# Attention scores on quarters of the PE array, queries and keys loaded as token x both heads, value copies on GpSimd

## The chip, the cores and the metric

One core of a Trainium2 chip runs the whole program in one launch. The metric is the device time of that launch in microseconds (us), the median of several runs. Five engines work from queues of their own, in order: TensorE (matmuls and transposes, into PSUM), VectorE and ScalarE (which empty PSUM and do the elementwise work), GpSimd (elementwise work in SBUF) and SyncE (SP), which here issues nearly all DMA transfers. PSUM has eight banks of 2 KB per partition. Semaphores tie the queues together; a buffer that is used again is such a tie too.

## The reference

Three parts follow one another; the change is in the first.

```python
def _attn_ref(q, k, v):                    # (4, 8, 576, 64) each, fp32
    scores = (1.0 / np.sqrt(D)) * np.matmul(q, k.transpose(0, 1, 3, 2))
    rel = pos[:, None] - pos[None, :]
    scores = np.where((rel >= 0) & (rel < 64), scores, -1e9)
    scores = scores - np.max(scores, axis=-1, keepdims=True)
    attn = np.exp(scores)
    attn = attn / (np.sum(attn, axis=-1, keepdims=True) + 1e-09)
    return np.matmul(attn, v)
```

Then 2304 tokens of 512 values are routed to 8 experts with 288 places each (two products with a ReLU between), and the result goes through a gated product with 1536 inner columns.

## The kernel before, in words

**Units and groups.** The window of 64 means that a block of 64 queries needs two blocks of 64 keys. A unit (b, c, hp) is one block c of 64 queries (nine in a sequence) of two heads, hp and hp + 4, in batch b. There are 144 units in the order batch, head pair, block, and four make a group g (36 groups). One turn i of the main loop (from line 346 on) does one step for each of several groups: scores(i), maxima(i), exponents(i-1), transposed(i-3), values(i-5), out_x(i-6), the preparations that a plan gives to this turn (take(i)), norms(i-1). Inside norms(i-1) stands negated(i), the negated maxima which the next exponentials need as a bias. The order of the lines is the order of each engine's queue.

**Loads and preparation.** load_rows brings 576 rows of queries or keys of both heads as 72 partitions with two tokens side by side. prep turns one head's rows with four transposes into a tile ps_t and copies it out with two copies of 64 partitions (even and odd tokens): keys on ScalarE into kt (L196), queries on VectorE (L198) into qbd, in which the two heads of a unit stand on the diagonal, with zeros beside them. load_v brings values to partitions 64 to 127 of vw, and copy_v moves them by DMA to partitions 0 to 63, one block later (L177), so that one matmul meets the previous and the present block of keys.

**Scores to outputs.** scores writes the mask (a matmul of 512 columns with the identity, L206) and adds four products of 128x128x128 (L210; in fp32 one product is two instructions). maxima is a reduction on VectorE (L216), exponents are four exponentials on ScalarE with sums (L226), norms are small operations on VectorE (L231, L219, L234) and a product on GpSimd (L238), transposed are four transposes into a ps_t tile (L243) and a copy on ScalarE (L251). values are eight products into two halves of the output's partitions (L259), out_x copies the outputs to xT on VectorE (L273). When 512 tokens of all heads are there, logits (L283, four column strips of the array) and logits2 (L295) make the routing's inputs.

**PSUM.** ps_s has two banks (scores), ps_t three (transposed probabilities and preparations, by turns), ps_o two (outputs), ps_l one (logits).

**The plan.** todo gives each half of a preparation its turn, at most two in a turn; loads gives each head pair's load its turn, by when buffers come free (three for raw queries and keys, six for vw). At the end of turn 27 (`if i == 3 * NC`) convert_move and st.load(4) issue seven loads of weights of 512 KB, on the same SP queue.

Of the kernel before, what the change touches and what calls it, by code (L numbers as in the profile page):

```python
# [7 lines left out]
F32 = mybir.dt.float32  # L8
# [60 lines left out]
class Kernel:  # L69
# [30 lines left out]
    def attention(self, ctx):  # L100
# [45 lines left out]
        def qbd(b, hp):  # L146
            return qbds[(b * HP + hp) % NQ]


        vws = [one.tile([128, NC, 2, D], F32, name=f"vw{i}") for i in range(NV)]  # L150
# [5 lines left out]


        units = [(b, c, hp) for b in range(B) for hp in range(HP) for c in range(NC)]
        groups = [units[4 * g:4 * g + 4] for g in range(len(units) // 4)]
        NG = len(groups)  # L160

        raw, kt = {}, {}
# [16 lines left out]
        def prep(name, b, hp, s):  # L179


            ps = ps_t.tile([128, 4, 72], F32, name="ps_t")
            for t in range(4):
                nc.tensor.transpose(ps[:, t, :], raw[name, b, hp][:, s, t], self.ident[0:72, 0:72])
            sl = slice(64 * s, 64 * s + 64)
            if name == "k":
                if not s:
                    kt[b, hp] = kt_p.tile([128, NC, 64], F32, name="kt")
                dst = kt[b, hp][sl]
            else:  # L190
                dst = qbd(b, hp)[sl, :, s, :]
            dst = dst.rearrange("r c (m e) -> r e c m", e=2)
            for e in range(2):
                x = ps[64 * e:64 * e + 64].rearrange("r t p -> r (t p)").rearrange("r (c m) -> r c m", c=NC)
                if name == "k":
                    nc.scalar.activation(dst[:, e], x, AF.Copy)  # L196
                else:
                    nc.vector.tensor_copy(dst[:, e], x)  # L198

        SS, PP, PN, PT, OO, SM = {}, {}, {}, {}, {}, {}  # L200

        def scores(g):
            ps = ps_s.tile([128, 4, 128], F32, name="ps_s")
            SS[g] = ps
            first = [4 - u for u, (b, c, hp) in enumerate(groups[g]) if c == 0] or [0]
            mm(ps, identb, mask[:, first[0]:first[0] + 4], start=True, stop=False)  # L206
            for u, (b, c, hp) in enumerate(groups[g]):
                k = kt[b, hp].rearrange("p c i -> p (c i)")
                kk = k[:, 64 * c - 64:64 * c + 64] if c else k[:, None, 0:64].to_broadcast([128, 2, 64])
                mm(ps[:, u, :], qbd(b, hp)[:, c].rearrange("p s i -> p (s i)"), kk, start=False, stop=u == 3)  # L210

# [40 lines left out]

        def values(g, late=False):
            ps = ps_s.tile([128, 4, 64], F32, name="ps_s") if late else ps_o.tile([128, 4, 64], F32, name="ps_o")
            OO[g] = ps
            for u, (b, c, hp) in enumerate(groups[g]):
                for s in range(2):
                    sl = slice(64 * s, 64 * s + 64)
                    mm(ps[sl, u, :], vw(b, hp)[:, c, s, :], PT[g][:, u, 64 * s:64 * s + 64],  # L259
                       start=True, stop=True)  # L260

        def out_x(g, late=False):
            ps, us = OO[g], groups[g]
            u = 0
            while u < 4:
                b, c, hp = us[u]
                n = 1
                while u + n < 4 and us[u + n] == (b, c + n, hp):
                    n += 1
                t0 = b * S + 64 * c  # L270
                dst = xT[:, hp, t0:t0 + 64 * n].rearrange("p (n i) -> p n i", n=n)
                if late:
                    nc.vector.tensor_copy(dst, ps[:, u:u + n])  # L273
                else:
                    nc.scalar.activation(dst, ps[:, u:u + n], AF.Copy)
                u += n

        LT = {}

        def logits(t0, n, ps_p=ps_l, name="ps_l", act=False):  # L280
# [9 lines left out]
        def logits2(t0, n, ps_p=ps_l, name="ps_l"):  # L290
            lt = LT[t0]
# [9 lines left out]
        def load(h):  # L301

            if h < NP:
                load_rows("q", h // HP, h % HP)
                load_rows("k", h // HP, h % HP)
            if 0 < h <= NP:
                load_v((h - 1) // HP, (h - 1) % HP)
            if 1 < h:
                copy_v((h - 2) // HP, (h - 2) % HP)

# [12 lines left out]
        for h in reversed(range(NP)):  # L323
            for a in (("k", 1), ("q", 1), ("k", 0), ("q", 0)):
                i = h * NC // 4 - 2 if h else -1
                if h == 1:
                    i = 0 if a[1] else -1
                while i > 0 and len(todo.get(i, ())) >= 2:
                    i -= 1
                todo.setdefault(max(i, -1), []).insert(0, (h, a))  # L330
        todo[-1].sort(key=lambda x: (x[0], x[1][1]))
        ready = {h: max(i for i, t in todo.items() for x in t if x[0] == h) for h in range(NP)}
        loads = {}
        for h in range(NR, NP + 2):

            i = max(ready[h - NR] if h < NP else 0, (h - NV) * NC // 4 + VL + 1 if h > NV else 0)
            loads.setdefault(i + 1, []).append(h)

        def take(i):
            for h, (name, s) in todo.get(i, ()):  # L340
                prep(name, h // HP, h % HP, s)

        warm = ps_l.tile([128, 512], F32, name="ps_l")
        self.warm(warm, 8)
        take(-1)
        done, late, window = 0, None, iter(())
        for i in range(NG - 1):
            for h in loads.get(i, ()):
                load(h)
            scores(i)  # L350
            maxima(i)
# [8 lines left out]
            if i >= VL + 1:  # L360
                if late:
                    logits2(*late)
                    if late[0] + late[1] == 128 * self.n0:
                        window = self.first_window(ps_l.tile([128, 1], F32, name="ps_l"))
                    late = None
                elif done < 1536 and S * ((i - VL - 1) // NC) >= done + 512:
# [13 lines left out]

        n = NG - 1
        list(window)
        scores(n)
        maxima(n)
        exponents(n - 1)
        negated(n)
        out_x(n - 6, True)
        norms(n - 1)
        transposed(n - 3, True)
        values(n - 5)  # L390
        exponents(n)
        out_x(n - 5, True)
        values(n - 4)
        norms(n, True)
        transposed(n - 2)
        values(n - 3, True)
        out_x(n - 4, True)
        transposed(n - 1)
        out_x(n - 3, True)
        transposed(n, 2)  # L400
        values(n - 2, True)
        values(n - 1)
        out_x(n - 2)
        out_x(n - 1, True)
        values(n)
        out_x(n)
# [4 lines left out]
        logits2(2048, 256)  # L411

# [735 lines left out]
```

## Time and profile before

| what | value |
|---|---|
| time, median of 3 runs | 842.52 us (841.31 to 843.17) |
| profiled execution: its own time | 840.74 us |
| its span | 839.0 us |
| granted TensorE clock, mean over the span | 0.981 |
| TensorE busy | 801.5 us (96%) |
| VectorE busy | 516.9 us (62%) |
| ScalarE busy | 396.3 us (47%) |
| GpSimd busy | 94.9 us (11%) |

The attention stage is the first 122 us of the span or so. The shares of the table are means over stages with different limits, so that stage has to be read by itself: first the busy time by stretch, then the engines' instructions in order of time. A row of the timeline has the start, the time until the last of its instructions ended, the engine, the line, the operation, the tile written and read, the shape, the count and, in brackets, idle time before it with what ended it. PE is TensorE, PEld its weight load, ACT ScalarE, DVE VectorE, POOL GpSimd.

### The profile page before, as it was taken

Reading aid. Unit: us, or ns where it says so; the run is one execution under the profiler, and the core shown is the slowest. Engines: PE = TensorE matmul, PEld = TensorE weight load, DVE = VectorE, ACT = ScalarE, POOL = GpSimd, SP = SyncE. Lnnn points to the kernel's source line nnn. Section 1 sums busy time; section 2 is a strip of 40 time slices with the busy share of each in tenths; the row PEclk is TensorE's granted clock in tenths of the full one; section 3 lists DMA queues with packets and bytes.
Section 4 is the critical chain, followed back from the end, with each engine's and each line's share of the span. In section 5 each row is a group of like instructions: output and inputs, shape, how many; then the busy total and the mean of one; then the engine's idle time right before and its main releaser. Section 6 shows DMA issues by size and latency. Waiting matters only on the chain.

```text
span 839.0 us, 14875 instructions
## 1 busy us (share of the span) xinstructions
PE 801.5 (96%) x5635; PEld 750.0 (89%) x5635; DVE 516.9 (62%) x1104; ACT 396.3 (47%) x998; POOL 94.9 (11%) x167
## 2 busy tenths in 40 slices
PE   7999986599999999999999999999999999999997
PEld 6888965499999999999888989999999999999996
DVE  6777868667777777788787844554443464443432
ACT  5989966346665665664343413433232243231311
POOL 6333323300000000000000000110000002000002
PEclk8999997699999999999999999999999999999999
DMA  8999916657877777786655322232112223201001
GB/s 185 194 190 202 261 49 219 195 167 249 258 263 241 251 239 235 242 240 200 221 159 172 100 103 75 101 126 77 36 41 76 75 87 140 71 15 67 1 1 75
DMA packets 92333, 123.72 MB, mean 147 GB/s; under 512 B 24417, under 2 KB 59233, under 8 KB 92257
## 3 DMA queue, kind: packets, MB, share of 16 engines
q1 hardware_dynamic: 89376, 113.28, 45.5%
q0 software_dynamic: 2880, 9.44, 3.2%
q8 instruction: 46, 0.75, 0.4%
q14 instruction: 31, 0.25, 0.1%
HBM read 99.63 MB, written 18.87 MB: 141 GB/s over the span
## 4 chain that ended last, share of the span: by engine, by line
PE 38%; issue 33%; DVE 6%; POOL 2%; ACT 1%; DMA 1%; POOLq 0%; DVEq 0%
PE psw L943 12%; PE psa L943 12%; PE psg L943 9%; PE pso L943 4%; DVE wlo L60 2%; POOL out_dram L1079 1%; PE psw L975 1%; DVE t L898 1%; DVE t L896 1%; DVE sg L1059 1%; DVE t L900 1%; ACT p L1061 1%; DVE sg L1056 1%; DVE t L894 0%; DMA wraw<-in_moe_w_dram 0%
## 5 line engine op out<-in xcount | busy, mean ns | idle before, releaser
L943 PE MATMUL psg<-y,whi 128*128 128x384 f32 x1152 | 223.1, 336 | 0.0
L943 PEld LDWEIGHTS psg<-y,whi 128*128 128x128 f32 x1152 | 201.6, 188 | 0.0
L60 DVE TENSOR_TENSOR wlo<-wraw,whi 128x512 fp32r<-128x512 f32 x236 | 149.7, 687 | 8.8 <-DVEq L674 3.8
L943 PE MATMUL pso<-whi,p 128*128 128x512 f32 x432 | 133.3, 390 | 0.0
L59 ACT ACTIVATE whi<-wraw 128x512 fp32r<-128x512 f32 x236 | 129.9, 620 | 2.9 <-ACTq L674 2.9
L943 PE MATMUL psg<-y,wlo 128*128 128x384 f32 x576 | 124.1, 337 | 4.4 <-DVE sg L1056 4.4
L1061 ACT ACTIVATE p<-sg 128x384 fp32r<-128x384 f32 x72 | 37.8, 525 | 161.5 <-DVE sg L1059 161.5
L943 PEld LDWEIGHTS psg<-y,wlo 128*128 128x128 f32 x576 | 102.2, 188 | 9.1 <-DVE sg L1056 6.5
L1056 DVE TENSOR_TENSOR sg<-sg,psg 128x384 f32<-128x384 f32 x72 | 39.8, 553 | 107.9 <-ACT sg L1055 107.8
L1055 ACT ACTIVATE sg<-psg 128x384 f32<-128x384 f32 x72 | 35.3, 490 | 134.2 <-PE psg L943 134.2
L943 PEld LDWEIGHTS pso<-whi,p 128*128 128x128 f32 x432 | 80.6, 188 | 14.5
L943 PE MATMUL pso<-wlo,p 128*128 128x512 f32 x216 | 84.2, 390 | 0.0
L943 PE MATMUL psw<-xt,whi 128*128 128x288 f32 x512 | 78.5, 295 | 0.0
L943 PE MATMUL psa<-hh,whi 128*128 128x288 f32 x256 | 75.5, 295 | 0.0
L943 PE MATMUL psa<-hl,whi 128*128 128x288 f32 x256 | 75.5, 295 | 0.0
L943 PE MATMUL psa<-hh,wlo 128*128 128x288 f32 x256 | 75.3, 294 | 0.0
L1059 DVE TENSOR_TENSOR sg<-sg,psg 128x384 f32<-128x384 f32 x72 | 39.9, 555 | 54.7 <-PE psg L943 53.1
L943 PEld LDWEIGHTS psw<-xt,whi 128*128 128x128 f32 x512 | 71.5, 188 | 0.0
L1079 POOL DMA_INDIRECT out_dram<-orow,idx x18 | 17.5, 972 | 461.0 <-ACT orow L1077 270.9
L1062 DVE TENSOR_TENSOR p<-sg,p 128x384 fp32r<-128x384 f32 x72 | 40.2, 559 | 42.6 <-ACT p L1061 42.6
L932 ACT ACTIVATE hh<-psw 128x288 fp32r<-128x288 f32 x64 | 26.3, 411 | 61.8 <-PE psw L943 60.5
L226 ACT ACTIVATE pp<-ps_s,nm 128x128 f32<-128x128 f32 x144 | 50.9, 365 | 5.0 <-DVE nm L219 4.2
(176 smaller groups left out, 1097.4 us busy)
## 6 DMA issues: line engine op xcount, KB each, us to landing
wraw<-in_moe_w_dram SPq DMA_DIRECT2D x64, 512.0 KB
wraw<-w SPq DMA_DIRECT2D x54, 512.0 KB
w<-t SPq DMA_DIRECT2D x36, 256.0 KB
raw<-in_moe_w_gate_dram SPq DMA_DIRECT2D x12, 512.0 KB
raw<-in_moe_w_val_dram SPq DMA_DIRECT2D x12, 512.0 KB
raw<-in_moe_w_out_dram SPq DMA_DIRECT2D x12, 512.0 KB
rawq<-in_q_dram SPq DMA_DIRECT2D x32, 144.0 KB
rawk<-in_k_dram SPq DMA_DIRECT2D x32, 144.0 KB
```

The costliest lines, as they stand in the source:

```text
L59: self.nc.scalar.activation(h[sl], t[sl], AF.Copy)
L60: self.nc.vector.tensor_tensor(lo[sl], t[sl], h[sl].bitcast(F32), op=OP.subtract)
L226: nc.scalar.activation(PP[g][:, u, :], ps[:, u, :], AF.Exp, bias=nm[:, u:u + 1], scale=scale, accum_out=SM[g][:, u:u + 1])
L896: nc.vector.scalar_tensor_tensor(t, hi, -0x40000000, t, op0=OP.bitwise_and, op1=OP.bitwise_or)
L932: nc.scalar.activation(h, x, AF.Relu)
L943: self.nc.tensor.matmul(acc, x, y, start=start and i == 0, stop=stop and i == len(seq) - 1)
L1055: nc.scalar.activation(sg, pg, AF.Sigmoid)
L1056: nc.vector.tensor_tensor(sg, sg, pg, op=OP.mult)
L1059: nc.vector.tensor_tensor(sg, sg, pv, op=OP.mult)
L1061: nc.scalar.activation(p[0][:, sl], sg, AF.Copy)
L1062: nc.vector.tensor_tensor(p[1][:, sl], sg, p[0][:, sl].bitcast(F32), op=OP.subtract)
L1079: d = nc.gpsimd.indirect_dma_start(out=self.out, out_offset=bass.IndirectOffsetOnAxis(ap=self.idx[:, 6 * g + t:6 * g + t + 1], axis=0), in ...
```

## The change

Scores are made for eight units (two groups) at a time, on a quarter of the array each: one head's 64 rows by one block's 64 queries. The two heads go to two PSUM banks, and a group g now holds one head of eight units, two in its partitions. qbd with its zeros is gone. A raw tile has 96 partitions and per token both heads' 64 values, so that one transpose of 96 tokens gives both heads; a preparation is half a sequence: three transposes and one copy of 128 partitions, on VectorE but for the second half of the keys, on ScalarE. Value copies are three GpSimd products with 1.0 per head pair. values and out_x work on eight units, in odd and even turns. ps_s has four banks, ps_t two, ps_o two with the logits among its tiles; vw has five buffers. The end after the loop is written anew. The core of the diff:

```diff
-        NR, NQ, NV, VL = 3, 4, 6, 5
+        NR, NV = 3, 5
-        ps_s, ps_t, ps_o, ps_l = pool("ps_s", 2, PS), pool("ps_t", 3, PS), pool("ps_o", 2, PS), pool("ps_l", 1, PS)
+        ps_s, ps_t, ps_o = pool("ps_s", 4, PS), pool("ps_t", 2, PS), pool("ps_o", 2, PS)
-        qbds = [one.tile([128, NC, 2, 64], F32, name=f"qbd{i}") for i in range(NQ)]
-        for i in range(NQ):
-            for s in range(2):
-                nc.gpsimd.memset(qbds[i][64 * s:64 * s + 64, :, 1 - s], 0.0)
...
-            t = raw[name, b, hp] = raw_p.tile([72, 2, 4, 2 * D], F32, name="raw" + name)
+            t = raw[name, b, hp] = raw_p.tile([96, 6, 2, D], F32, name="raw" + name)
             for s in range(2):
-                nc.sync.dma_start(t[:, s], src[b, HP * s + hp].rearrange("(t p e) d -> p t (e d)", p=72, e=2))
+                nc.sync.dma_start(t[:, :, s, :], src[b, HP * s + hp].rearrange("(t p) d -> p t d", p=96))
...
-        def copy_v(b, hp):
-            nc.sync.dma_start(vw(b, hp)[0:64, 1:NC], vw(b, hp)[64:128, 0:NC - 1])
+        def copy_v(b, hp, i):
+            v, c0, c1 = vw(b, hp), 3 * i + 1, min(3 * i + 4, NC)
+            nc.gpsimd.tensor_tensor(v[0:64, c0:c1], v[64:128, c0 - 1:c1 - 1],
+                                    vone[64:128].to_broadcast([64, c1 - c0, 2, D]), op=OP.mult)
+        def prep(name, b, hp, x):
+            if name == "v":
+                copy_v(b, hp, x)
+                return
+            if not x:
+                tr[name, b, hp] = kt_p.tile([128, S], F32, name=name + "t")
+            ps = ps_t.tile([128, 3, 96], F32, name="ps_t")
+            for t in range(3):
+                nc.tensor.transpose(ps[:, t, :], raw[name, b, hp][:, 3 * x + t].rearrange("p s d -> p (s d)"),
+                                    self.ident[0:96, 0:96])
+            dst = tr[name, b, hp][:, 288 * x:288 * x + 288].rearrange("p (t i) -> p t i", t=3)
+            if name == "k" and x:
+                nc.scalar.activation(dst, ps, AF.Copy)
             else:
+                nc.vector.tensor_copy(dst, ps)
+        def scores(G):
+            us = units[8 * G:8 * G + 8]
+            for h in range(2):
+                SS[2 * G + h] = ps_s.tile([128, 4, 128], F32, name="ps_s")
+            for r in range(2):
+                first = ([4 - m for m in range(4) if us[2 * m + r][1] == 0] or [0])[0]
+                for h, sl in enumerate(sides):
+                    mm(SS[2 * G + h][sides[r]], identb[sl, sl], mask[sl, first:first + 4], start=True, stop=False)
+            for m in range(4):
+                for r in range(2):
+                    b, c, hp = us[2 * m + r]
+                    for h, sl in enumerate(sides):
+                        k = tr["k", b, hp][sl]
+                        kk = k[:, 64 * c - 64:64 * c + 64] if c else k[:, None, 0:64].to_broadcast([64, 2, 64])
+                        mm(SS[2 * G + h][sides[r], m, :], tr["q", b, hp][sl, 64 * c:64 * c + 64], kk,
+                           start=False, stop=m == 3)
+        def values(G, j0=0, n=8, p=ps_o, name="ps_o"):
+            ps = OO[G, j0] = p.tile([128, n, 64], F32, name=name)
+            for j in range(j0, j0 + n):
+                b, c, hp = units[8 * G + j]
+                for h, sl in enumerate(sides):
+                    mm(ps[sl, j - j0, :], vw(b, hp)[:, c, h, :], PT[2 * G + h][:, j // 2, sides[j % 2]],
                        start=True, stop=True)
...
-                i = h * NC // 4 - 2 if h else -1
-                if h == 1:
-                    i = 0 if a[1] else -1
+                i = 2 * ((h * NC + 4 * a[1]) // 8) - (1 if h < 2 else 2)
                 while i > 0 and len(todo.get(i, ())) >= 2:
                     i -= 1
                 todo.setdefault(max(i, -1), []).insert(0, (h, a))
...
+        for h in range(NP):
+            for x in range(3):
+                todo.setdefault(min(2 * ((h * NC + 3 * x) // 8) + 1, NG - 2), []).append((h, ("v", x)))
-        for h in range(NR, NP + 2):
-            i = max(ready[h - NR] if h < NP else 0, (h - NV) * NC // 4 + VL + 1 if h > NV else 0)
+        for h in range(NR, NP + 1):
+            i = max(ready[h - NR] if h < NP else 0, 2 * (((h - NV) * NC - 1) // 8) + 6 if h > NV else 0)
             loads.setdefault(i + 1, []).append(h)
...
-            scores(i)
+            if i % 2 == 0:
+                scores(i // 2)
             maxima(i)
             if i >= 1:
                 exponents(i - 1)
...
             if i >= 3:
                 transposed(i - 3)
-            if i >= VL:
-                values(i - VL)
+            if i % 2 and i >= 5:
+                values((i - 5) // 2)
+            if late:
+                logits2(*late)
...
+            if i % 2 == 0 and i >= 6:
+                if done < 1536 and S * (8 * (i - 6) // 2 // (HP * NC)) >= done + 512:
                     late = (done, 512)
                     logits(*late)
                     done += 512
-                out_x(i - VL - 1, True)
+                out_x((i - 6) // 2)
             take(i)
```

out_x copies on VectorE in both versions of the loop; after the loop the scores of the last group are not made any more, since those of two groups are made in turn 34, and values and out_x of the last 16 units go in halves of four units.

## Rows read from the trace of the kernel before

**Rows 1.** Busy time by stretch: us, PE, PEld, DVE, ACT, POOL, clock, DMA, GB/s.
```profile
84.00:106.30 22.30, 21.70 (x286) 19.53 (x285) 18.52 (x65) 21.43 (x88) 8.32 (x8) 1.00 0.91 252
```
**Rows 2.** Timeline of TensorE, one turn: start, us, engine, line, operation.
```profile
61.99 0.38 PE L206 MATMUL ps_s<-mask,identb 128*128 128x512 bf16 x1 [0.22 <-ACT pp L226]
62.21 1.05 PE L210 MATMUL ps_s<-kt,qbd 128*128 128x128 f32 x8
63.10 0.60 PE L243 MATMUL ps_t<-ident,pn 128*128 128x128 f32 x4
63.63 0.69 PE L259 MATMUL ps_o<-pt,vw 128*64 128x64 f32 x16
64.25 0.47 PE L184 MATMUL ps_t<-ident,rawq 72*128 72x72 f32 x4
...
64.80 0.38 PE L206 MATMUL ps_s<-mask,identb 128*128 128x512 bf16 x1
```
**Rows 3.** Timeline of ScalarE, one turn (exponentials two and three left out).
```profile
60.44 0.37 ACT L226 ACTIVATE pp<-ps_s,nm 128x128 f32<-128x128 f32 x1 [0.33 <-DVE nm L219]
...
61.83 0.60 ACT L251 ACTIVATE pt<-ps_t 128x512 f32<-128x512 f32 x1
62.30 0.87 ACT L196 ACTIVATE kt<-ps_t 64x288 f32<-64x288 f32 x2
63.20 0.37 ACT L226 ACTIVATE pp<-ps_s,nm 128x128 f32<-128x128 f32 x1
```
**Rows 4.** Timeline of VectorE in the same turn.
```profile
61.56 0.92 DVE L198 COPY qbd<-ps_t 64x288 f32<-64x288 f32 x2
62.41 0.15 DVE L231 TENSOR_SCALAR sm<-sm 128x4 f32<-128x4 f32 x1
62.47 0.16 DVE L219 TENSOR_SCALAR nm<-nm 128x4 f32<-128x4 f32 x1
```
**Rows 5.** Timeline of the start: fifth preparation, last one ahead of the loop, first mask.
```profile
7.30 0.33 PEld L184 LDWEIGHTS ps_t<-ident,rawq 72*128 72x128 f32 x4 [0.30 <-ACT kt L196]
...
8.96 0.71 PE L184 MATMUL ps_t<-ident,rawk 72*128 72x72 f32 x4 [1.18 <-DMA rawk<-in_k_dram]
...
9.47 0.63 PE L206 MATMUL ps_s<-mask,identb 128*128 128x512 bf16 x1
```
**Rows 6.** Timeline of ScalarE: first exponential of groups 3, 31, 32 and 34.
```profile
21.82 0.37 ACT L226 ACTIVATE pp<-ps_s,nm 128x128 f32<-128x128 f32 x1
...
104.80 0.37 ACT L226 ACTIVATE pp<-ps_s,nm 128x128 f32<-128x128 f32 x1
...
106.75 0.37 ACT L226 ACTIVATE pp<-ps_s,nm 128x128 f32<-128x128 f32 x1
...
113.42 0.37 ACT L226 ACTIVATE pp<-ps_s,nm 128x128 f32<-128x128 f32 x1 [0.43 <-DVE nm L219]
```
**Rows 7.** Timeline of TensorE: the third logits of the loop.
```profile
108.60 1.07 PE L283 MATMUL ps_l<-big,wgp 128*32 128x512 f32 x8
```
**Rows 8.** Groups by line, 18.2 to 112.5 us: busy us, mean ns, idle before.
```profile
L238 POOL TENSOR_TENSOR pn<-pp,sm 128x512 f32<-128x512 f32 x32 | 33.3, 1039 | 59.4 <-DVE sm L234 30.4 <-PE ps_s L210 14.1 <-PE ps_t L243 4.4
...
L288 DVE COPY lt<-ps_l 128x512 f32<-128x512 f32 x3 | 2.1, 691 | 4.2 <-PE ps_l L283 4.2
```
**Rows 9.** DMA packets and share of 16 engines, 44.2 to 45.2 and 23.1 to 24.1 us.
```profile
DMA packets 310, 0.16 MB, mean 159 GB/s; under 512 B 73, under 2 KB 304, under 8 KB 310
q1 hardware_dynamic: 310, 0.16, 82.2%
...
DMA packets 559, 0.21 MB, mean 213 GB/s; under 512 B 265, under 2 KB 559, under 8 KB 559
q1 hardware_dynamic: 559, 0.21, 109.7%
```
**Rows 10.** Timeline of SP: first of the weights, first transfer behind them.
```profile
90.16 1.33 SPq L875 DMA_DIRECT2D raw<-in_moe_w_gate_dram  x2
...
97.10 3.08 SPq L173 DMA_DIRECT2D vw<-in_v_dram  x2
```

More of the change, by code (lines that the diff above doesn't have):

```diff
@@ L158, in attention @@
         units = [(b, c, hp) for b in range(B) for hp in range(HP) for c in range(NC)]
-        groups = [units[4 * g:4 * g + 4] for g in range(len(units) // 4)]
-        NG = len(groups)
-        raw, kt = {}, {}
+        NG = len(units) // 4
+        sides = slice(0, 64), slice(64, 128)
+        vone = one.tile([128, 1, 1, 1], F32, name="vone")
+        nc.vector.memset(vone, 1.0)
+        raw, tr = {}, {}
         def load_rows(name, b, hp):
             src = self.k if name == "k" else self.q
-            t = raw[name, b, hp] = raw_p.tile([72, 2, 4, 2 * D], F32, name="raw" + name)
+            t = raw[name, b, hp] = raw_p.tile([96, 6, 2, D], F32, name="raw" + name)
             for s in range(2):
-                nc.sync.dma_start(t[:, s], src[b, HP * s + hp].rearrange("(t p e) d -> p t (e d)", p=72, e=2))
+                nc.sync.dma_start(t[:, :, s, :], src[b, HP * s + hp].rearrange("(t p) d -> p t d", p=96))
         def load_v(b, hp):
@@ L173, in load_v @@
                 nc.sync.dma_start(vw(b, hp)[64:128, :, s, :], self.v[b, HP * s + hp].rearrange("(c p) d -> p c d", p=64))
-        def copy_v(b, hp):
-            nc.sync.dma_start(vw(b, hp)[0:64, 1:NC], vw(b, hp)[64:128, 0:NC - 1])
[L179 to L189, printed above, removed]
-            else:
[L191 to L198, printed above, removed]
@@ L200, in attention @@
-        SS, PP, PN, PT, OO, SM = {}, {}, {}, {}, {}, {}
[L202 to L210, printed above, removed]
+        def copy_v(b, hp, i):
+            v, c0, c1 = vw(b, hp), 3 * i + 1, min(3 * i + 4, NC)
+            nc.gpsimd.tensor_tensor(v[0:64, c0:c1], v[64:128, c0 - 1:c1 - 1],
+                                    vone[64:128].to_broadcast([64, c1 - c0, 2, D]), op=OP.mult)
@@ L251, in transposed, with out_x, logits @@
                 nc.scalar.activation(PT[g], ps, AF.Copy)
[L253 to L259, printed above, removed]
+        def values(G, j0=0, n=8, p=ps_o, name="ps_o"):
[4 more added lines that the diff above has]
+                    mm(ps[sl, j - j0, :], vw(b, hp)[:, c, h, :], PT[2 * G + h][:, j // 2, sides[j % 2]],
                        start=True, stop=True)
-        def out_x(g, late=False):
-            ps, us = OO[g], groups[g]
+        def out_x(G, j0=0, n=8, act=False):
+            ps, us = OO[G, j0], units[8 * G + j0:8 * G + j0 + n]
             u = 0
-            while u < 4:
+            while u < n:
                 b, c, hp = us[u]
-                n = 1
-                while u + n < 4 and us[u + n] == (b, c + n, hp):
-                    n += 1
+                k = 1
+                while u + k < n and us[u + k] == (b, c + k, hp):
+                    k += 1
                 t0 = b * S + 64 * c
-                dst = xT[:, hp, t0:t0 + 64 * n].rearrange("p (n i) -> p n i", n=n)
-                if late:
-                    nc.vector.tensor_copy(dst, ps[:, u:u + n])
-                else:
-                    nc.scalar.activation(dst, ps[:, u:u + n], AF.Copy)
-                u += n
+                dst = xT[:, hp, t0:t0 + 64 * k].rearrange("p (n i) -> p n i", n=k)
+                if act:
+                    nc.scalar.activation(dst, ps[:, u:u + k], AF.Copy)
+                else:
+                    nc.vector.tensor_copy(dst, ps[:, u:u + k])
+                u += k
         LT = {}
-        def logits(t0, n, ps_p=ps_l, name="ps_l", act=False):
+        def logits(t0, n, ps_p=ps_o, name="ps_o", act=False):
             ps = ps_p.tile([128, n], F32, name=name)
@@ L379, in attention @@
                 self.st.load(4)
-        n = NG - 1
+        n, N = NG - 1, NG // 2 - 1
         list(window)
-        scores(n)
         maxima(n)
@@ L386, in attention @@
         negated(n)
-        out_x(n - 6, True)
         norms(n - 1)
         transposed(n - 3, True)
-        values(n - 5)
+        values(N - 2)
+        logits2(*late)
         exponents(n)
-        out_x(n - 5, True)
-        values(n - 4)
+        out_x(N - 2)
         norms(n, True)
         transposed(n - 2)
[L396 to L399, printed above, removed]
+        values(N - 1, 0, 4)
+        transposed(n - 1, True)
+        values(N - 1, 4, 4)
+        out_x(N - 1, 0, 4)
         transposed(n, 2)
[L401 to L406, printed above, removed]
+        out_x(N - 1, 4, 4)
+        values(N, 0, 4, ps_s, "ps_s")
+        values(N, 4, 4)
+        out_x(N, 0, 4)
+        out_x(N, 4, 4, True)
         list(self.wants_first(self.n0, 12))
@@ L410, in attention @@
         logits2(1536, 512, ps_o, "ps_o")
[L411 removed]
+        logits2(2048, 256, ps_s, "ps_s")
     def rows_setup(self, ctx):
```

23 lines of the change are left out of this document (7 added, 16 removed).

## The prediction, made before the changed kernel was run

> **What bounds the kernel now.** The change touches the attention stage alone, so I read the views of that stage, first the table of busy time by stretch. In its last part [rows 1] TensorE is busy 21.70 of 22.30 us and ScalarE 21.43, VectorE 18.52, GpSimd 8.32, at clock 1.00: two engines are full at once. Then the timeline by engine, over one turn of the loop (one group g of four units). TensorE [rows 2]: mask at 61.99, scores, four transposes of probabilities, values, transposes of queries and keys, next mask at 64.80. A turn is 2.81 us and each item follows the last at once. ScalarE [rows 3]: four exponentials (call them E) from 60.44, the copy of transposed probabilities (P, L251) at 61.83, two key copies at 62.30, the next E at 63.20: 2.76 us without a hole. VectorE [rows 4] has some slack. So a gain needs both TensorE and ScalarE to get shorter, and nothing new to tie them together. I follow the time from E to E: E(3) starts at 21.82 and E(34) at 113.42 [rows 6], 91.6 us for 31 turns.
>
> **Scores.** Before, 8 instructions of 128 columns take 1.05 us per group after a mask of 0.22 (61.99 to 62.21) [rows 2]. After, two groups are made together: 32 instructions of 128 columns, 4096 in all, and four masks. The trace shows no matmul on halves of the rows, so I bound it from rows that split columns. Values, on two column halves, take 0.69 us for 16x64 columns where the scores take 1.05 for as many [rows 2]; less the 0.23 to 0.28 that the last one needs to finish, that is twofold. Logits, on four strips, take 1.07 us for 8x512 = 4096 columns [rows 7]: fourfold. If quarters behave like strips, two groups cost 0.2 (gap) + 0.22 + 0.9 = 1.3 us and not 2.2; if only the column halves overlap, 2.4. I take 1.3, since a quarter, like a strip, has its own weights and its own outputs, and the two row halves write different banks.
> The Trainium skill, "TensorEngine Tiling (Array Packing)", Key Properties, says that the four 64x64 tiles run independently but that changing the mode drains the engine; by it the scores also take 1.3 us. No run here shows the row half of that sentence.
>
> **Copies.** Per head pair ScalarE had 4 key copies and VectorE 4 query copies on 64 partitions, 0.43 to 0.46 us each [rows 3, 4]. Now there are 4 copies on 128 partitions with as many columns: one on ScalarE, three on VectorE. ScalarE's work falls from 2.76 to about 2.05 us a turn. TensorE transposes 3x96 columns instead of 4x72, as many, and 12 instead of 16 blocks a head pair with twice the copies saved: no change of its 0.47 us. VectorE in an even turn then has maxima and outputs of 512 columns, 0.69 each like another copy of as many [rows 8], two copies 0.92 [rows 4], and small ones of 0.4 or so: 2.7 us.
>
> **The buffers, which decide.** ps_t goes from 3 to 2 buffers. Its tiles come in the order T (probabilities), q, k in each turn. That buffers go round in order is seen at the start: the fifth preparation waited for ScalarE's copies of the second [rows 5], two short of three buffers plus one. With three, k took the buffer of the last turn's k, long free. With two, k takes the buffer of the T of its own turn, so TensorE must wait for P; P stands behind E on ScalarE; and the next E stands behind k's copy. This is a ring with one turn per round, and every step has a row:
> - E starts to P starts: 60.44 to 61.83 = 1.39; P lasts 0.60 [rows 3]; to TensorE 0.04 (estimate, as after the ScalarE copies in rows 5).
> - k's transposes until their copy can start: 0.47 + 0.03 [rows 2].
> - second half of the keys, copied by ScalarE: 0.45 until the next E (0.90 for two [rows 3]). Ring: 2.98.
> - first half, copied by VectorE: 0.39 until the sums (61.56 + 0.46 to 62.41), 0.22 to the end of the negation, 0.1 to E [rows 4]: 0.71. Ring: 3.24.
> Both exceed 2.81, whatever the engines' sums are. The plan in the code gives two preparations to 25 of the turns 4 to 34: 13 end with a second half, 12 with a first. Turns 5, 13, 23, 31 and 33 have none; there the step is that of 104.80 to 106.75, 1.95 [rows 6].
> Even turns: T ends 2.2 us after the keys' transposes began in the turn before (0.22 + 1.3 + 0.09 + 0.33 + 0.27); E ends after 2.3 to 2.6; so scores at 1.3 us do not lengthen the ring.
> Sum E(3) to E(34): 13x2.98 + 12x3.24 + 5x1.95 = 87.4; the last step, with logits and no preparation, 3.75. Logits stay in two other turns: VectorE's copy of 512 columns (0.69) waits for logits that take 1.07 us after T and stands ahead of the outputs and the query copy, which then ends at 3.2 + 0.69 + 0.69 + 0.45 = 5.0 us of the turn, and E follows at 5.3 and not 4.2: +1.1, and +1.4 where the keys' copy is on VectorE too. Total 93.6 against 91.6: **+2.0 us**.
>
> **Start.** The first mask, at 9.47, waited 1.18 us for the second pair's keys [rows 5], which the first scores no longer need. But the fourth pair's loads, which turn 3 needs, come no faster: -1.5 us, from -2 to 0. The memsets of qbd leave GpSimd; nobody waited for them, 0.
>
> **Loads.** Queries and keys now come in pieces of 256 B as values do, and not 512 B. In one stretch with 73 of 310 packets under 512 B the queues moved 0.16 MB at 82.2%, in another with 265 of 559 0.21 MB at 109.7% [rows 9]: bytes per busy share 0.195 and 0.191 MB, so small pieces cost almost nothing by themselves: 0 to 2%, beside other work. The 16 value copies (256 KB each) leave the queue, whose share was 0.91 [rows 1]: room, no time.
> With five value buffers instead of six, the last head pair's load moves from turn 27 to turn 29 of the order, behind the weights issued at the end of turn 27 (seven transfers of 512 KB, issued from 90.16 to 97.10 [rows 10]). At 252 GB/s [rows 1] their 3.67 MB take 14.6 us. SP can issue them once the thirteenth pair's values have a buffer, at turn 25; the last keys land after 1.3 (issue of those values) + 14.6 + 2.8 (576 KB of queries and keys) = 18.7 us, and the preparation in turn 30 is due after 1.2 + 3x3.24 + 2x2.98 = 16.9. **+1.5 us**, from 0 to 4.
>
> **Value copies on GpSimd.** 48 multiplications of 64x384. No row crosses partitions; by the 1039 ns of 128x512 [rows 8] one is 0.78 us (estimate), from 0.65 to 1.6. With the normalization 1.04 + 1.33x0.78 = 2.1 us a turn of 3.1: hidden, as the transposes use a result two turns later. At 1.6 us that cover is gone.
>
> **Tail.** The last scores are already made, but the values of the last two groups wait for both transposes and the outputs of eight units stand ahead of the last sums on VectorE: +0.8 us, from 0 to 1.5.
>
> **Sum.** 2.0 - 1.5 + 1.5 + 0.8 = +2.8 us on the profiled execution's 840.74 us: 843.5. The median shown lies 1.8 above it: **845 us**, own range 840 to 851.
>
> **Rivals.**
> (B) Row halves do not overlap. Scores of two groups take 1.1 us more; T's end (2.2 + 1.1) then follows E's, so each pair of turns grows by 0.75 to 1.0: 17 x 0.9 = 15 us, 861 us (median). For: no row shows row halves together. Against: logits.
> (C) Faster: the ring does not close, because P is done when TensorE comes to k. Place: the k transposes (L184); price: TensorE's own work, 1.3 + 0.53 (T) + 0.69 (q, k) = 2.5 us in an even and 0.53 + 1.07 (values of eight units) + 0.69 = 2.3 in an odd turn, 2.4 against 2.81. Over 25 turns that saves 10 us, with the start 11.5: 831. It decides as soon as E starts some 0.7 us earlier against TensorE than the order of the queues lets me see. Against: the fifth preparation's wait [rows 5]; for: the sums of all four engines, below 2.5 us a turn.
> (D) GpSimd's copies cost 1.6 us, or hold up VectorE's small operations (sums, negation) which stand in the ring. With 0.6 us in 13 odd turns: +8, 853.
>
> **Chances.** Forecast 0.52 (0.40 of it slower, 0.12 within 0.2% of 842.5), B 0.12, C 0.20, D 0.08, others 0.08 (0.05 same, 0.03 faster). About 0.2% is what a measurement of this kernel can tell from no change. Faster 0.23, same 0.17, slower 0.60. The range, 829 to 857, takes in the forecast, D and most of C, and leaves out B and the fast end of C.
>
> **What would show it.** Right: TensorE waits before the k transposes with P (the ScalarE copy of transposed probabilities) as releaser, about 0.4 to 0.9 us in most turns; E to E 2.98 and 3.24 by turns, 1.95 where nothing is prepared; TensorE and ScalarE both with holes. Two groups' scores in about 1.1 us. A wait for the last queries or keys near turn 30. Wrong: E to E below 2.7 us with no such wait (C), scores of two groups near 2.2 us (B), VectorE's sums that take 0.5 us beside GpSimd copies (D).

## The result and the profile after

The changed kernel takes 851.40 us (850.74 to 851.73); the kernel before, run beside it, 842.85 (841.31 to 844.37). The ratio is 1.011, 95% interval 1.0094 to 1.0126: slower by 8.55 us. The profiled execution is one of 850.74 us, its span 848.9 against 839.0, its mean granted clock 0.969 against 0.981.

First the view that answers to [rows 1], the busy time in the same stretch of the attention stage (us, PE, PEld, DVE, ACT, POOL, clock, DMA, GB/s), of the changed kernel:

```profile
84.00:106.30 22.30, 16.75 (x280) 12.82 (x273) 14.15 (x46) 14.36 (x64) 12.35 (x15) 1.00 0.76 218
```

No engine is full any more: TensorE 16.75 of 22.30 us where it had 21.70, ScalarE 14.36 where it had 21.43. Both got shorter, and yet the turn got longer. So something ties them together. In the view of waits, from 10 to 126 us (engine, line, what it waited for, us in total, times, longest), TensorE's longest entries, one for its weight loads and one for its matmuls, name it:

```profile
PEld ps_t L184 <- ACT pt L251: 13.4, 15, 1.8
...
PE ps_t L184 <- ACT pt L251: 9.0, 14, 1.4
```

That is the key transposes waiting for P, the ScalarE copy of transposed probabilities. One turn of it in the timeline, TensorE and ScalarE (exponentials two to four left out):

```profile
71.31 0.37 ACT L226 ACTIVATE pp<-ps_s,nm 128x128 f32<-128x128 f32 x1 [1.42 <-DVE nm L219]
...
72.69 0.61 ACT L251 ACTIVATE pt<-ps_t 128x512 f32<-128x512 f32 x1
...
73.36 0.47 PE L184 MATMUL ps_t<-ident,rawk 96*128 96x96 f32 x3 [0.85 <-ACT pt L251]
...
73.86 0.41 ACT L188 ACTIVATE kt<-ps_t 128x288 f32<-128x288 f32 x1 [0.56 <-PE ps_t L184]
74.17 0.36 ACT L226 ACTIVATE pp<-ps_s,nm 128x128 f32<-128x128 f32 x1
74.41 0.63 PE L243 MATMUL ps_t<-ident,pn 128*128 128x128 f32 x4 [0.59 <-ACT kt L188]
```

Read it as a circle: E at 71.31, P at 72.69 (1.38 later), the key transposes at 73.36 (0.67), their copy at 73.86 (0.50), the next E at 74.17 (0.31): 2.86 us, in which TensorE waits 0.85 and then 0.59, and ScalarE 0.56.

Where the 10 us between the two spans lie, by the starts of E (E(g) is the first exponential of group g) and later marks: E(3) is 0.65 us earlier (21.17 against 21.82), E(3) to E(34) takes 98.6 us and not 91.6 (+7.0), E(34) to the last sum of logits +0.9, from there to the first routing count +0.5, the six routing counts until the ranks begin +2.4, all the rest of the span -0.2.

### The profile page after: what moved, and what is told of

Read it like the earlier page. It is cut to its first block, busy times and chain, and to the rows that moved or that the text cites. A ratio compares the mean times of both kernels' runs of the same rounds, so it can differ in the third digit from the quotient of the medians.

```text
span 848.9 us, 15315 instructions
## 1 busy us (share of the span) xinstructions
PE 793.9 (94%) x5895; PEld 732.9 (86%) x5895; DVE 509.0 (60%) x1078; ACT 375.4 (44%) x947; POOL 125.7 (15%) x206
## 4 chain that ended last, share of the span: by engine, by line
PE 38%; issue 33%; DVE 6%; POOL 1%; ACT 1%; DMA 0%; POOLq 0%; DVEq 0%; ACTq 0%
PE psw L940 12%; PE psa L940 12%; PE psg L940 8%; PE pso L940 4%; DVE wlo L60 2%; POOL out_dram L1076 1%; PE psw L972 1%; DVE t L893 1%; DVE t L895 1%; DVE sg L1056 1%; ACT p L1058 1%; DVE t L897 1%; DVE t L891 1%; DVE sg L1053 1%; PE psw L434 0%
```

## The experiments

The third column is the ratio to the kernel before, run on the same chip, with its 95% interval; the last two are of the profiled execution. Where the intervals of two rows overlap, as those of e3, e4, e5, e9, e10 and e12 do with the changed kernel's, that of e6 with e2's and those of e7, e8 and e11 with one another, the medians alone don't tell the two kernels apart, and the reading rests on the traces.

| kernel | median us | ratio | E(3) to E(34) | mean clock |
|---|---|---|---|---|
| before (three sets of 13 to 15) | 841.9 to 842.3 | 1 | 91.6 | 0.981 |
| changed | 851.40 | 1.0110 (1.0094 to 1.0126) | 98.6 | 0.969 |
| e1: before, two banks | 855.93 | 1.0168 (1.0151 to 1.0185) | 104.5 | 0.985 |
| e2: changed, three banks | 842.74 | 1.0007 (0.9994 to 1.0020) | 91.8 | 0.976 |
| e3: changed, copy first | 849.85 | 1.0081 (1.0051 to 1.0110) | 96.1 | 0.962 |
| e4: changed, few value copies | 848.31 | 1.0083 (1.0059 to 1.0108) | 97.1 | 0.977 |
| e5: changed, weights later | 849.84 | 1.0099 (1.0075 to 1.0123) | 95.0 | 0.973 |
| e6: e2, few value copies | 841.56 | 0.9988 (0.9975 to 1.0002) | 88.0 | 0.972 |
| e7: e2, weights later, normalization first | 837.39 | 0.9947 (0.9930 to 0.9963) | 87.2 | 0.974 |
| e8: e2, weights later, copies by transfer | 835.63 | 0.9935 (0.9911 to 0.9960) | 83.7 | 0.983 |
| e9: changed, one head behind the other | 854.74 | 1.0158 (1.0124 to 1.0191) | 102.1 | 0.973 |
| e10: changed, filled tail | 853.63 | 1.0142 (1.0116 to 1.0169) | 97.5 | 0.974 |
| e11: e8, filled tail | 839.22 | 0.9969 (0.9953 to 0.9984) | 84.5 | 0.978 |
| e12: e8, two banks | 850.06 | 1.0098 (1.0065 to 1.0131) | 95.1 | 0.971 |

**The ring, e1, e2 and e12.** e1 puts it into the kernel before, which has nothing else of the change.

```diff
-... pool("ps_t", 3, PS) ...
+... pool("ps_t", 2, PS) ...
```

> The kernel before with one number changed: two ps_t banks and not three. Theory (ring): the key transposes of a turn must wait for the ScalarE copy of the same turn's transposed probabilities, and the next exponentials stand behind the key copies. By the kernel before's rows a turn with a key preparation then lasts 1.39 + 0.60 + 0.04 + 0.50 + 0.90 = 3.43 us from E to E and not 2.81; there are some 25 such turns, so +0.62 x 25 = +15 us: about 858 us, and TensorE waits in L184 for ScalarE's pt. Rival (two banks are enough, and the turn is set by the engines' sums): E to E stays within 0.1 us of 2.81 and the time within 2 us of 842.5.

The turns with a preparation, but for the four beside logits or first values, took 3.43 to 3.47 us (3.43 were expected); the whole took 13.8 us more. The waits, over 10 to 126 us:

```profile
PEld ps_t L184 <- ACT pt L251: 16.5, 25, 1.3
```

Twenty-four of the 25 turns have the wait, and one turn before them has it too. The ring is shown, and so is its length, worked out from rows in which it did not yet exist.

```diff
-... pool("ps_s", 4, PS), pool("ps_t", 2, PS) ...
+... pool("ps_s", 3, PS), pool("ps_t", 3, PS) ...
```

> The changed kernel with the eight banks dealt out otherwise: ps_t three, ps_s three (not two and four). Nothing else is changed. Theory (ring): the key transposes take a bank that was free a turn ago, the wait of TensorE for pt at L184 (9.0 + 13.4 us in the changed kernel) goes, and a turn falls from 2.85 and 3.36 us to what the engines need, 2.4 to 2.6 us: over 25 turns 12 to 18 us less, of which the wait for the last queries and keys takes some back, since the DMA does not get faster: 836 to 843 us. Rival (VectorE, held up by GpSimd's value copies, sets the turn): E to E stays above 2.9 us and the time within 3 us of 851.

One bank moved from scores to transposes gives 8.7 us back. But the turns don't fall to 2.4 everywhere: E(3) to E(34) is 91.8, an ordinary turn about 2.7, and the view of waits has a new first entry on TensorE, the transposes of probabilities behind GpSimd:

```profile
PEld ps_t L243 <- POOL pn L238: 12.6, 13, 1.3
```

e12 asks the same in the other direction, in e8 below, where neither GpSimd nor the weights play a part. Its edit is that of e2 undone.

> The kernel with value copies by transfer and the weights at turn 33, with the banks of the changed kernel (ps_t two, ps_s four) and not three and three. It measures the ring in a kernel where GpSimd and the weights no longer play a part. Theory (the ring is the largest term): a turn with a preparation is back at 2.85 and 3.36 us, E(3) to E(34) at 94 to 96 us against 83.7 with three banks, the time 845 to 848 us; by the changed kernel it gains 4 to 6 us (turns without a preparation at 1.95, turn 30 at 3.3). Rival (three banks only paid because of GpSimd's copies and the transfers): within 3 us of 835.6.

The ring costs 14.4 us there (850.06 against 835.63; 13.7 by the two ratios). Turns without a preparation took 1.94 to 1.99 us and turn 30 3.35, while the ordinary turns of the ring took 2.70 to 3.46 as in the changed kernel: the two other terms are gone, the ring is not. By the changed kernel e12 gains only 1.3 us in the median, less than the 4 to 6 expected, though E(34) comes 3.1 us earlier (116.68): behind E(34) the profiled execution lost 2.2 us of that on the changed kernel's, at a lower clock, see below.

**The order on ScalarE, e3.**

```diff
-            if i >= 1:
-                exponents(i - 1)
-            else:
-                negated(i)
             if i >= 3:
                 transposed(i - 3)
+            if i >= 1:
+                exponents(i - 1)
+            else:
+                negated(i)
```

> The changed kernel with two banks as it is, but in each turn ScalarE copies the transposed probabilities before the four exponentials and not behind them; TensorE's order is unchanged. Theory (ring): the copy that TensorE waits for no longer stands behind the exponentials, so the ring of E, copy, key transposes, key copy, E is cut without another bank; ScalarE's own sum 0.60 + 1.39 + 0.45 = 2.44 us is left: 25 turns at 2.5 to 2.7 us, 10 to 16 us less, the time 836 to 843 us, as with three banks. Rival (the exponentials now wait behind a copy that waits for TensorE's scores and transposes): turns of 2.9 us or more, 849 to 855 us.

A miss: the time is the rival's, though the turns are not 2.9 us throughout but mostly about 3.5 and 2.0 to 2.3 by turns. ScalarE's queue is in order, so now E stands behind a copy that waits for TensorE:

```profile
ACT pt L251 <- PE ps_t L243: 32.8, 24, 4.7
```

Here another buffer opened the ring (e2); another order of the queue only closed it elsewhere.

**GpSimd's copies, e4, e6 and e7.** e4 leaves 33 of the 48 copies out.

```diff
             if name == "v":
-                copy_v(b, hp, x)
+                if b * HP + hp < NV:
+                    copy_v(b, hp, x)
                 return
```

> The changed kernel without the GpSimd value copies of head pairs 5 to 15 (33 of 48 copies; these pairs meet the values of an earlier pair in half of the rows, so that part of the computation is left out). It measures what the copies cost VectorE: the sum of the norms (L231) takes 286 ns in the mean beside them and 164 in the kernel before, up to 790. Theory (ring with VectorE's small operations in it): those go back to 160 to 200 ns; a turn with a first half of the keys or with no preparation gets 0.1 to 0.5 us shorter, in all 2 to 6 us, 845 to 849 us; turns that end with a key copy on ScalarE hardly change. Rival (the small operations are off the path): within 1 us of 851.

By groups of instructions, 10 to 126 us (busy us, mean ns, idle before), the copies and VectorE's sums in the changed kernel, and then the sums in e4 (a line further down there):

```profile
L172 POOL TENSOR_TENSOR vw<-vw,vone 64x384 f32<-64x384 f32 x32 | 26.0, 826 | 2.0 <-DMA vw<-in_v_dram 1.1
L231 DVE TENSOR_SCALAR sm<-sm 128x4 f32<-128x4 f32 x36 | 10.3, 286 | 5.9 <-ACT pp L226 5.9
```

```profile
L232 DVE TENSOR_SCALAR sm<-sm 128x4 f32<-128x4 f32 x36 | 6.7, 187 | 6.7 <-ACT pp L227 6.7
```

Turns 13, 23, 31 and 33, which have no preparation, fell from 2.35, 2.60, 2.35 and 2.31 to 1.94, 1.93, 1.99 and 1.94, 1.8 us in the sum; turn 5, whose copies stayed, is as long as before (2.61). The ordinary turns of the ring did not change by 0.03 us. Part of it was given back in turns 24 (+0.7) and 34 (+0.4). The median is 3.1 us lower, but in the profiled execution only 1.5 of it lies between E(3) and E(34); another 1.5 lies in the routing counts, where the clock was higher.

> The changed kernel with three ps_t and three ps_s banks, as in the run before that gave 842.7 us, and besides without the value copies of head pairs 5 to 15 (so that half of the rows meet an earlier pair's values there). With two banks the leaving out of these copies gave about 3 us. Theory (with the ring open, GpSimd is the next bound: the transposes of probabilities wait 12.6 us for the normalization, which stands behind value copies on GpSimd, and the small operations of VectorE are stretched): that wait falls under 4 us, turns without a preparation go to 1.95 us and the others to about 2.4; 5 to 10 us less than with three banks alone, 833 to 838 us. Rival (the sums of ScalarE, VectorE and TensorE near 2.5 us are the bound): 1 to 3 us less, 840 to 842.

e6 is e2 and e4 together. The sums took 186 ns, the wait for the normalization fell from 12.6 to 4.8 us, and E(3) to E(34) by 3.75: the mechanism is there, but the time fell by 1.2 us, as the rival had it. Turn 30 grew from 6.22 to 7.20 us (the last queries and keys, which a faster loop wants earlier still), and from E(34) to the last sum of logits it took 11.81 us (10.49 in e2), part of it at a granted clock of 0.57.

e7 takes up both with all the work kept:

```diff
-            if i == 3 * NC:
+            if i == 31:
...
                 norms(i - 1)
+            take(i, True)
```

(take(i) makes the preparations as before, take(i, True) the value copies, now behind the normalization; banks as in e2.)

> The changed kernel with three ps_t and three ps_s banks, the weights issued at the end of turn 31, and in each turn the normalization issued to GpSimd ahead of the value copies. All of the work is kept. Theory (queue order on GpSimd and on the transfer queue): the transposes' wait for the normalization (12.6 us with three banks alone) halves, 2 to 4 us; turn 30 goes from 6.22 to about 3.5 us, 2.5 us: 836 to 839 us. Rival (the normalization's input comes as late as before, since the sums on VectorE are held up by the copies whatever their order): only the weights' part, 840 us.

837.39 us, inside the expected 836 to 839; turn 30 at 3.04, the transposes' wait for the normalization at 1.5 us and not 12.6. What each of the two edits gives by itself was not run with three banks.

**The weights, e5.** Only the first of e7's edits, in the changed kernel.

> The changed kernel with the weights' transfers (seven of 512 KB) issued at the end of turn 31, behind the loads of the last queries, keys and values, and not at the end of turn 27, ahead of them. Theory (the last head pair's rows wait behind the weights): turn 30, 5.53 us from E to E in the changed kernel with TensorE waiting 1.59 us for rawq and 0.88 for rawk, falls to 3.0 to 3.4 us, and its time by 2 to 2.5 us: 849. The weights are first used at 132 us of the profile and land by about 124: no new wait. Rival (the queues are slow there whatever the order, since 4.4 MB are due at once): turn 30 stays above 4.5 us, and the time within 1 us of 851.

Turn 30 fell from 5.53 to 3.34 us, turn 32 from 3.30 to 2.86, E(34) came 3.5 us earlier. Yet the median fell by 1.6 only. Two lines of the tail's timeline, of e5 and of the changed kernel, show one cause, the clock; it is the same instruction:

```profile
120.64 1.12 PE L243 MATMUL ps_t<-ident,pn 128*128 128x128 f32 x4
```

```profile
123.80 0.65 PE L243 MATMUL ps_t<-ident,pn 128*128 128x128 f32 x4
```

The granted clock in e5 was 0.61 from 120.2 to 124.2 us, 1.00 in the same place of the changed kernel (123.7 to 127.7); from E(34) to the last sum of logits e5 took 11.95 us and not 10.49.

**Copies by transfer, e8: the lowest median.** With three banks the value copies go back to the SP queue, one load step behind the values (as copy_v before), and the weights go to turn 33.

```diff
-            nc.gpsimd.tensor_tensor(v[0:64, c0:c1], v[64:128, c0 - 1:c1 - 1], ...)
+            nc.sync.dma_start(vw(b, hp)[0:64, 1:NC], vw(b, hp)[64:128, 0:NC - 1])
...
-            if i == 3 * NC:
+            if i == 33:
```

> The changed kernel with three ps_t and three ps_s banks, value copies by transfer on the SP queue as in the kernel before (one load step after the values), and the weights issued at the end of turn 33. All of the work is kept. Theory (GpSimd's copies cost more than the transfers they replace, once the ring is open): small operations of VectorE back to 165 to 200 ns, GpSimd at 1.04 us a turn; ordinary turns 2.4 to 2.5 us; less 5 to 8 us, but the queues carry 256 KB more per head pair, so that turns near loads wait for rawq and rawk: 834 to 840 us. Rival (the transfers become the bound): waits for rawq, rawk and vw of 10 us or more in the sum, 843 us or more.

835.63 us: faster than both kernels and than e2, but not told apart from e7's 837.39. The sums take 163 ns again. Two turns with preparations take 4.8 to 5.9 us together, mostly 5.1 to 5.3, a little more than the 2.4 to 2.5 a turn expected; TensorE is at 19.43 of 22.30 us in the stretch of [rows 1]; the queues are at 0.88 and 244 GB/s there, as before (0.91 and 252).

**The quarters, e9.**

```diff
-            for m in range(4):
-                for r in range(2):
-                    b, c, hp = us[2 * m + r]
-                    for h, sl in enumerate(sides):
+            for h, sl in enumerate(sides):
+                for m in range(4):
+                    for r in range(2):
+                        b, c, hp = us[2 * m + r]
```

> The changed kernel with the scores of one head's eight units issued first and those of the other head behind them, so that in the queue a row half of the array follows itself and only the column halves alternate. It measures what the overlap of the row halves is worth (rival B of the prediction). Theory (TensorE's queue is in order, so the two row halves no longer run beside each other): the 32 instructions take about 2.0 us and not 1.04, the transposed probabilities of even turns end 1 us later, behind the exponentials, and 17 pairs of turns grow by 0.75 to 1.0 us: 13 to 17 us more, 864 to 868 us. Rival (TensorE has holes of that size at the wait for the ScalarE copy, and the ring takes the loss in): scores at 2.0 us as well but the time within 4 us of 851.

The scores of two groups in the timeline, the changed kernel first and then e9:

```profile
70.62 1.04 PE L209 MATMUL ps_s<-kt,qt 64*64 64x128 f32 x32
```

```profile
48.90 1.54 PE L209 MATMUL ps_s<-kt,qt 64*64 64x128 f32 x32
```

1.54 us and not the 2.0 that both sides expected, and the time +3.3 us: the rival's time. 17 times 0.50 us would be 8.5; TensorE's holes take most of it in.

**Behind the loop, e10 and e11.** The same edit in the changed kernel and in e8: a tile of ps_s and four times `self.warm(fill, 2)` behind the loop.

> The changed kernel with eight matmuls of 512 columns, which nobody reads, issued to TensorE in pairs at four places behind the loop (where it waits). It is for the last part of the loss: behind the last exponentials of the loop the changed kernel loses another 3.7 us on the kernel before until the routing counts end, and there the granted clock is at half from 136 to 172 us but for a few stretches, at half from 132 to 163 in the kernel before with more stretches at full. Theory (TensorE's holes behind the loop bring the clock down early): the clock stays full some microseconds longer and the time falls by 2 to 4 us: 847 to 849. Rival (the clock falls by the routing's own holes later on, whatever stands in the tail): 0 to 1 us more for the matmuls, 851 to 852.

> The kernel with three ps_t and three ps_s banks, value copies by transfer and the weights at turn 33 (835.6 us), with the same eight matmuls behind the loop. Theory (holes behind the loop bring the clock down): 2 to 3 us less, 833 us, and less spread between executions (833 to 839 without them). Rival (routing's own holes): 835 to 837 us and the same spread.

Both medians are higher, by 2.2 and 3.6 us (2.9 by the ratios of e8 and e11); the mean clock was no better (0.971 over the four executions of e10 as of the changed kernel, 0.974 over the ten of e11 against 0.977 over the six of e8), and the spread no smaller (837.5 to 843.2 for e11). Some 3 us came in at one place far from the edit: behind a branch, where the gathered rows are waited for, TensorE stood still in the middle of eight matmuls that are in every kernel. e10:

```profile
167.09 1.44 PE L439 MATMUL psw<-identb 128*128 128x512 bf16 x3 [3.89 <-PEq L676]
...
170.74 2.29 PE L439 MATMUL psw<-identb 128*128 128x512 bf16 x5 [2.21 <-issue]
```

In the twelve profiles without this edit the eight follow one another in 3.2 to 3.6 us. "issue" is time in which nothing that the profile shows was waited for, so the row has the place and the 2.21 us, not the cause. With that the edit measures two things at once, and the tail's holes are neither confirmed nor excluded; no gain was seen.

## Why the prediction was right, and where not

The forecast was 845 us in a range of 829 to 857, slower as the likeliest sign. The sign and its cause hold; the size was 6 us short. The sum made +2.8 us of the profiled execution, and it was +10. The 7.2 us between them are turns without a preparation 2.5, the clock in the routing counts 2.2, loads 1.1, start 0.9, tail 0.7 and the last turn 0.3 (4.10 us where 3.75 was forecast), less 0.5 in the ring and the logits. All but the last of these erred the same way; +2.8 us is not much more than the 0.2% that by the prediction a measurement can tell from no change, so that the sign came out this clearly is in part luck.

**The ring.** Right, with its place and its wait. By classes of turns: keys' second half 2.87 us where 2.98 was forecast (the next E starts 0.31 behind the start of the key copy, not 0.45 [rows 3]); first half 3.30 in even turns (3.24 forecast) and 3.46 in odd ones. One link was wrong: only in even turns do the key transposes wait for P. In odd turns eight units' values (1.15 us) stand before them, P is done, and the waits are others: the keys' for the query copy (0.55) or the probabilities' for the key copy (0.59 at 74.41). Two banks close a circle there too, of nearly the same length; which bank each tile takes, and so why these are the waits, no run shows.

**Turns without a preparation.** The mis-sized term. From [rows 6] they were put at 1.95; they took 2.31 to 2.60, five of them +2.5 us. The step that failed is "hidden", said of the value copies because no transpose waits for their result. The price lay on another engine: VectorE's sum of 128x4 elements, 164 ns in the mean before, did not end before the GpSimd operation beside it. In turn 13 of the changed kernel, which has no preparation:

```profile
50.19 2.19 POOL L172 TENSOR_TENSOR vw<-vw,vone 64x384 f32<-64x384 f32 x3
...
50.47 0.58 DVE L231 TENSOR_SCALAR sm<-sm 128x4 f32<-128x4 f32 x1 [0.98 <-ACT pp L226]
...
51.21 0.37 ACT L226 ACTIVATE pp<-ps_s,nm 128x128 f32<-128x128 f32 x1 [0.36 <-DVE nm L219]
```

The first of the three copies ends at 51.02, the sum at 51.05, and the next E waits for the negation behind it. All eleven sums of the changed kernel that took over 220 ns end 25 to 29 ns behind a GpSimd operation, ten of them behind a value copy; in the kernel before and in e8 no sum is so long. The five sums of the turns without a preparation (0.53 to 0.84 us) exceed 164 ns by 2.5 us together, as much as these turns exceed 1.95. The reciprocal of the same shape took 177 or 178 ns beside GpSimd operations too. The Trainium skill, "SBUF — State Buffer", SBUF: two separate sides, says that GpSimd and a VectorE operation in a mode that takes two ports, or with two inputs in SBUF, lock each other out for a whole instruction, whichever starts first; these rows agree, though none shows in which mode the sum runs. Rival D named this mechanism, at 8 us for 13 odd turns; it is 2.5 us in five turns. In turns 11 and 29 the sum took 0.80 and 0.79 us and the turn 2.92, as in e4 without these copies (2.92 and 2.91): they end with a key copy on ScalarE, and by the prediction's own ring the sum does not stand in such a turn.

**Loads.** +1.5 us forecast, from 0 to 4 (its own terms, 18.7 against 16.9, make 1.8); e5 shows 2.6 (2.19 in turn 30, 0.44 in turn 32). What the smaller pieces cost, no run takes apart: in the stretch of [rows 1] the queues moved 218 GB/s at a share of 0.76, where they had moved 252 at 0.91, no fewer bytes for the same share.

**Start.** -1.5 forecast; E(0) came 2.6 us earlier, E(3) only 0.65. The second pair's keys, which the first scores no longer need, were waited for all the same a turn later (1.20 us for rawk, at 13.16). One execution says little here: in four profiles with the same start (changed, e4, e5, e10) E(3) lies between 20.32 and 21.49.

**Logits.** +1.1 and +1.4 forecast; the two turns took 3.97 and 3.69 us, +1.1 and +0.4.

**Tail.** +0.8 forecast, from 0 to 1.5; measured 0.9 to the last sum, and 0.5 more because the routing's first twelve transposes, which started at 122.56 ahead of the last sum in the kernel before, now wait for it (0.32 us, until 130.29).

**The term that was missing** is TensorE's clock behind the loop. From 16 to 32 us behind the first routing count the two profiled executions stand so, before and then changed (columns as in [rows 1]):

```profile
140.00:156.00 16.00, 7.67 (x111) 6.40 (x109) 13.61 (x54) 7.57 (x23) 4.58 (x10) 0.66 0.66 215
```

```profile
148.00:164.00 16.00, 9.55 (x104) 8.28 (x102) 12.59 (x51) 7.35 (x23) 4.95 (x10) 0.50 0.65 215
```

Nearly the same work, at 0.66 of full speed and at 0.50, that is, in the second wholly at 1.2 GHz. What that costs stands in the routing counts. From one matmul `low` to the next is a step, and each holds twelve transposes of rows, whose ScalarE copies stand ahead of other work of ScalarE and VectorE and of the next `low`. One step of each kernel, before and then changed, the transposes and the next `low`:

```profile
139.76 1.54 PE L427 MATMUL rowps<-ident,big 128*128 128x128 f32 x12
...
143.67 0.16 PE L620 MATMUL low<-sat,w 33*128 33x8 bf16 x1 [0.39 <-DVE sat L616]
```

```profile
153.01 2.83 PE L424 MATMUL rowps<-ident,big 128*128 128x128 f32 x12
...
157.90 0.16 PE L617 MATMUL low<-sat,w 33*128 33x8 bf16 x1 [1.31 <-DVE sat L613]
```

The first step took 4.06 us, its transposes at a clock of 1.00, the second 5.03, at 0.50. So it is in all fourteen profiles: transposes wholly at full clock go with 4.03 to 4.10 us (one step of e1 took 5.46), wholly at half with 5.02 or 5.03. The five steps took 21.49 us before, one of them with transposes of 2.8 us, and 23.74 in the changed kernel, three of them so: +2.2 us.

How far the medians differ by it is an estimate. Six executions of e8 run from 833.25 us at a mean clock of 0.983 to 839.51 at 0.971; 42 of the kernel before have 0.980 in the mean, four of the changed one 0.971. From the slopes within the sets of ten or more executions of one kernel (1.8 to 3.3 us per 0.01) that makes 1.6 to 3 us of the 8.55. What takes the clock away earlier is open: e10 and e11 didn't settle it, and e12, whose clock was 0.66 from 4 to 8 us behind E(34) and whose last four steps were wholly at half, lost part of its gain there.

**Rivals.** B did not come: 32 score instructions took 1.04 us, as long as 8 had, and four masks 0.41 together, so the four quarters overlap fourfold. C needed the ring open; e7 and e8, where it is open and the other two terms are mended, gave 837 and 836, still 5 to 6 us above its 831, at about 2.6 us a turn (e8) and not 2.4.

## What to carry to other kernels

When two engines are full and a change relieves both, look for the circle that they form through their buffers, and add up its steps from rows: one PSUM bank more or less for the transposes was worth 8.7 to 14.4 us here. Work moved to an idle engine is not hidden because nobody waits for its result: look also at the small operations of other engines beside it, which took up to 0.84 us here where they had taken 0.16. A loop that gets faster asks for its loads earlier, so look at what stands ahead of them in the queue (turn 30 took 5.53 us, 6.22 in e2 and 7.20 in e6, and 3.0 to 3.4 with the weights behind the loads).

## What was not expected of the hardware

- The order of issue decides how far quarters of the array overlap: with one head behind the other, 32 instructions of 128 columns took 1.54 us where they take 1.04 with the row halves by turns. The estimate for column halves alone was 2.0; no run shows where the difference comes from.
- With eight matmuls more behind the attention loop there was a hole of 2.21 us (e10) and 2.04 us (e11) in TensorE's work some 40 to 50 us later, behind a branch, and in none of the other twelve profiles; its cause is not shown.
- The clock behind the loop differs from kernel to kernel and from execution to execution by several microseconds' worth, and it took back part of what e5, e6 and e12 had gained. A routing step with its twelve transposes at half clock took 0.9 to 1.0 us longer than one at full.
